# Another issue order for the attention stage, and six small instructions of the start on other engines

## The chip, the cores and the metric

The kernel runs on one core of one Trainium2 chip. The metric is the device time in microseconds (us) of one execution; the median of three runs is given for the kernel before. The core has five engines that run side by side, each with a queue that it works off strictly in order: TensorE (PE, matrix products and transposes; PEld is its weight load), VectorE (DVE), ScalarE (ACT), GpSimd (POOL) and SyncE (SP, which here only issues DMA transfers).

## The reference

Two stages, cut to what matters (B = 8 batches, H = 8 heads, S = 576 positions, D = 64, factor = 4, so 144 pooled positions):

```python
q_d = q.reshape(B, H, Sd, factor, D).mean(axis=3)   # k_d, v_d alike
out_d = sm_attn(q_d, k_d, v_d)                       # dense attention over 144 pooled positions
out_up = np.repeat(out_d, factor, axis=2)
mask = np.abs(pos[:, None] - pos[None, :]) < factor  # a band of 7 positions
attn = softmax(where(mask, scale * q @ k.T, -1e9))
x = out_up + attn @ v                                # -> 4608 tokens of 512 numbers
# second stage: each token goes to the best of 8 experts, if its skip score is above 0
h = np.maximum(xc[mask] @ w1[e], 0.0)
y[mask] = gate_w[mask, None] * (h @ w2[e])
out[do_compute] = xc + y
```

## The kernel before

**Attention.** The 4608 tokens are worked off in 36 tiles of 128 rows; a tile holds four groups of 32 positions with all 8 heads, and 4.5 tiles make a batch. A tile passes these steps, each a small function: `scores` (PE: four matmuls lay the mask into a PSUM bank `S`, 16 add the products), `s_max`, `s_sub` (DVE, from PSUM into `Et`), `s_exp` (ACT), `s_sum`, `recip` (DVE), `norm` (POOL, into `Nt`), `p_transpose` (PE), `p_evac` (ACT), `up_mm` and `values` (PE, into a bank `O`), `x_out` (ACT), `store_x` (a DMA), `x_transpose` (PE), `x_evac` (ACT), and the router's `logits`. Each batch also has its pooled attention: `pool_q`, `pool_k`, `pool_v` and `pool_vr` add four neighbours each, `d_scores` (PE, five of them into a bank `Sd`; n = 0 to 3 is a pair of heads each) is followed by `d_max` (DVE), `d_neg` and `d_exp` (ACT), `d_transpose`, `d_values` and so on. Each of the PSUM banks `S`, `Sd`, `T` and `O` exists twice: the third `scores` in the order waits until `s_sub` of the first has read its bank.

**Routing.** Every 16 tiles (and for the last four) the steps `r_...` count which token goes to which expert. `r_row` (DVE, L671) writes a tile `Am` that exists once, and `r_lists` (PE, 4 matmuls) reads it. At the end `slots` (L690) writes the list `gix`, and GpSimd gathers the first expert's rows by it. **The second stage** then runs expert by expert, written out in code that the change leaves alone.

**What sets the order.** All calls of the first stage, loads among them, are collected in a list of 1235 nodes (`node(...)`), and the table `ORDER` says in which order they are called. A manual schedule keeps that order on every engine and on the DMA queue of SP, so the table alone decides what stands in front of what. Semaphores are put in where data or a buffer asks for them.

The places that the change and the steps below touch: `pool_v` (L242 to L247) adds the four value rows of a batch in three adds; `pool_q0` (L260 to L272) pools the queries of batch 0, pairs 0 and 2 by one reduction on DVE and pairs 1 and 3 by three adds on POOL, and copies the last 16 columns behind the others; L766 is the helper `copy`, which casts the identity to `idb` and the mask to `mk`, both of which every `scores` needs; `zero_k` (L228, by `fill`, L184) zeroes the parts of the key buffers that no load writes, halves `hh` = 0 on ACT or DVE, 1 on POOL; `load_k` (L221), `load_q` (L208) and `load_v4` (L236) issue the loads, the first batch's keys in four pieces of 288 KB, its queries in two of 576 KB, its values in one of 512 and one of 640 KB.

```python
    def copy(eng, t, src):
        (eng.copy if eng is nc.scalar else eng.tensor_copy)(out=t, in_=src)
...
    for k in ORDER:
        fn, args = nodes[k]
        fn(*args)
```

Of the kernel before, what the change touches and what calls it, by code (L numbers as in the profile page):

```python
# [52 lines left out]


ORDER = (
# [61 lines left out]
)  # L117

@with_exitstack
def tile_attention_moe(ctx, tc, qT, kT, vW, v4, mask, cst, ups, cid, w9, w1, w2, out):
    nc = tc.nc
    NB = qT.shape[0]
# [114 lines left out]


    def pool_v(b, k):  # L242
        eng = nc.gpsimd if b else nc.vector
        if k == 0:
            B[b]["vd"] = dp.tile([128, D], F32, name="vd")
        vd, V4 = B[b]["vd"], B[b]["V4"][:, :4 * D].rearrange("p (r d) -> p r d", r=4)
        eng.tensor_add(out=vd, in0=V4[:, 0] if k == 0 else vd, in1=V4[:, k + 1])  # L247
# [21 lines left out]
        else:  # L269
            nc.gpsimd.tensor_add(out=qd, in0=qv[:, :, 0] if k == 0 else qd, in1=qv[:, :, k + 1])  # L270
        if k in (None, 2):
            eng.tensor_copy(out=s["qd"][:, p, SD:], in_=qd[:, 128:])  # L272

    def pool_q(b, k):
        s = B[b]
# [506 lines left out]
        node(load_q, 0, slice(2 * c, 2 * c + 2))  # L782
        for hh in range(2):
            node(load_k, 0, hh, 2 * c, 2)
    node(copy, nc.vector, idb, ident)
    node(copy, nc.scalar, mk, mkf)
    for i in range(2):
        node(fill, nc.scalar, VBs[0][:, i])
# [443 lines left out]
```

## Time and profile before

| what | us |
|---|---|
| runs: median (lowest to highest) of 3 | 467.70 (466.41 to 469.99) |
| the profiled execution, by its own time | 462.81 |
| its span, from the first to the last instruction | 461.0 |
| first matmul of TensorE | 10.84 |
| first list of rows (`gix`) written | 206.12 to 206.30 |

The profile is that of one execution. Its busy times are what an engine spends inside instructions; "idle <- X" and the waits name the instruction that ended an idle time. The attention stage runs from the start to about 206 us; the rest is the second stage.

### The profile page before, as it was taken

To read this page: it belongs to the slowest core of one execution; us is meant where nothing else is said; L and a number is where in the kernel's file an instruction comes from. 1 tells how busy PE (TensorE), PEld (TensorE's weight loads), DVE (VectorE), ACT (ScalarE), POOL (GpSimd) and SP (SyncE) were. 2 spreads that over 40 slices of the span, in tenths; PEclk is the share of its full clock that TensorE was granted. 3 is DMA by queue.
4 is the path that set the end of the run, shared out by engine and by line. 5 is a ranking of instruction groups with operands and counts; after the bars stand their busy time and mean duration, and the time that the engine had idled before them with its cause. 6 is when DMAs were issued, how large, how long until landed. Compare 5 with 4: busy or idle time off the path is not lost.

```text
span 461.0 us, 13595 instructions
## 1 busy us (share of the span) xinstructions
PE 431.7 (94%) x5593; PEld 368.7 (80%) x5593; DVE 314.2 (68%) x572; ACT 252.9 (55%) x583; POOL 170.0 (37%) x200
## 2 busy tenths in 40 slices
PE   0879999999899999989999999999999999999994
PEld 0657787787788688866989899898989898998993
DVE  5989999786888868774656556456776655666422
ACT  6666787878687787624643443343646334454320
POOL 8747884656838542107002204105040220201002
PEclk9999999999999999989999999999999999999999
DMA  8988888988887778636754644635667564455201
GB/s 276 323 262 280 282 268 276 309 260 304 273 279 213 221 228 257 206 129 179 256 159 153 226 143 138 240 113 206 240 207 240 199 224 138 164 179 186 91 3 57
DMA packets 27110, 96.67 MB, mean 210 GB/s; under 512 B 4245, under 2 KB 4629, under 8 KB 24618
## 3 DMA queue, kind: packets, MB, share of 16 engines
q1 hardware_dynamic: 23186, 84.36, 56.6%
q0 software_dynamic: 3840, 11.09, 6.4%
q8 instruction: 64, 1.05, 0.9%
q14 instruction: 20, 0.16, 0.1%
HBM read 81.20 MB, written 15.73 MB: 210 GB/s over the span
## 4 chain that ended last, share of the span: by engine, by line
issue 46%; PE 28%; POOL 9%; DVE 8%; DMA 4%; ACT 3%; POOLq 1%; SPq 0%; DVEq 0%
PE O L195 12%; PE T L198 7%; POOL xr L959 4%; PE Sd L195 4%; PE S L195 4%; POOL out L959 4%; DVE KD L288 2%; DMA cs<-cst 2%; DMA out<-Y,six 1%; DMA mkf<-mask 1%; ACT KB L186 1%; DVE nm L423 1%; ACT Ed L322 1%; POOL Nt L446 1%; DVE r L439 1%
## 5 line engine op out<-in xcount | busy, mean ns | idle before, releaser
L959 POOL DMA_INDIRECT out<-Y,six x24 | 24.3, 1011 | 190.8 <-DVE Y L1030 187.6
L993 PE MATMUL ph<-xth,w1h 128*128 128x384 f32 (+2 forms) x256 | 80.8, 316 | 0.7 <-PEq L1058 0.4
L993 PE MATMUL ph<-xth,w1l 128*128 128x384 f32 (+2 forms) x256 | 78.9, 308 | 0.0
L993 PE MATMUL ph<-xtl,w1h 128*128 128x384 f32 (+2 forms) x256 | 78.4, 308 | 0.0
L1022 PE MATMUL py<-w2h,hh 128*128 128x512 f32 (+1 forms) x168 | 64.9, 387 | 0.4
L1022 PE MATMUL py<-w2h,hl 128*128 128x512 f32 (+1 forms) x168 | 64.9, 386 | 0.0
L1022 PE MATMUL py<-w2l,hh 128*128 128x512 f32 (+1 forms) x168 | 64.9, 386 | 0.0
L1001 ACT ACTIVATE hh<-ph 128x384 fp32r<-128x384 f32 x64 | 30.9, 492 | 57.6 <-PE py L1022 26.5
L1002 DVE SCALAR_TENSOR_TENSOR hl<-ph,hh 128x384 fp32r<-128x384 f32 x64 | 34.6, 553 | 37.0 <-ACT hh L1001 35.3
L993 PEld LDWEIGHTS ph<-xth,w1h 128*128 128x128 f32 x256 | 48.1, 188 | 1.9 <-issue 1.6
L993 PEld LDWEIGHTS ph<-xtl,w1h 128*128 128x128 f32 x256 | 48.0, 188 | 0.4
L993 PEld LDWEIGHTS ph<-xth,w1l 128*128 128x128 f32 x256 | 48.1, 188 | 0.0
L710 DVE TENSOR_TENSOR w2l<-raw,w2h 128x1024 fp32r<-128x1024 f32 x32 | 39.1, 1221 | 10.5 <-ACT w2h L709 10.5
L288 DVE TENSOR_REDUCE KD<-KB 128x288 f32<-128x1152 f32 (+1 forms) x36 | 42.9, 1207 | 4.6 <-DMA KB<-kT 4.5
L983 ACT CAST xth<-Tx 128x512 fp32r<-128x512 f32 x22 | 12.9, 587 | 58.4 <-PE Tx L978 58.3
L748 DVE TENSOR_TENSOR w1l<-raw,w1h 128x1024 fp32r<-128x1024 f32 x30 | 36.7, 1224 | 7.9 <-ACT w1h L743 7.7
L709 ACT CAST w2h<-raw 128x1024 fp32r<-128x1024 f32 x32 | 33.6, 1051 | 14.4 <-PE py L1022 12.6
L446 POOL TENSOR_TENSOR Nt<-Et,r 128x304 f32<-128x304 f32 x36 | 26.1, 731 | 37.6 <-PE T L198 9.5
L984 DVE TENSOR_TENSOR xtl<-Tx,xth 128x512 fp32r<-128x512 f32 x22 | 15.2, 691 | 34.2 <-ACT xth L983 31.5
L195 PE MATMUL O<-VB,PT 126*32 126x128 f32 x1152 | 37.8, 275 | 0.3 <-issue 0.3
L1022 PEld LDWEIGHTS py<-w2h,hh 128*128 128x128 f32 x168 | 31.5, 188 | 6.7 <-issue 1.2
L1022 PEld LDWEIGHTS py<-w2h,hl 128*128 128x128 f32 x168 | 31.5, 188 | 6.5
(160 smaller groups left out, 937.3 us busy)
## 6 DMA issues: line engine op xcount, KB each, us to landing
raw<-w SPq DMA_DIRECT2D x62, 512.0 KB
VB<-vW SPq DMA_DIRECT2D x36, 336.0 KB
Q<-qT SPq DMA_DIRECT2D x16, 576.0 KB
out<-X SPq DMA_DIRECT2D x36, 256.0 KB
KB<-kT SPq DMA_DIRECT2D x14, 576.0 KB
V<-v SPq DMA_DIRECT2D x8, 640.0 KB
V<-v SPq DMA_DIRECT2D x8, 512.0 KB
KB<-kT SPq DMA_DIRECT2D x4, 288.0 KB
```

Source lines behind the costliest of these rows:

```text
L195: last[:] = [nc.tensor.matmul(*args, **kw)]
L198: last[:] = [nc.tensor.transpose(*args)]
L288: i = nc.vector.tensor_reduce(out=kd, in_=kv, axis=AX.X, op=ALU.add)
L446: nc.gpsimd.tensor_tensor(out=Ns[i % NNS][:, :, :KW, :2], in0=TT[i]["E"], in1=heads(TT[i]["r"])[:, :, None, :].to_broadcast([128, 4, KW, 2 ...
L709: nc.scalar.copy(out=hf, in_=raw)
L710: nc.vector.tensor_tensor(out=flat(lo), in0=raw, in1=hf.bitcast(F32), op=ALU.subtract)
L748: nc.vector.tensor_tensor(out=flat(lo), in0=raws[e, j], in1=flat(hi).bitcast(F32), op=ALU.subtract)
L959: ins = nc.gpsimd.indirect_dma_start(bounds_check=NOUT - 1, oob_is_err=False, **kw).ins
L993: nc.tensor.matmul(P[i][:, :n], lhsT=a[:, c, 128 * i:128 * i + 128], rhs=bb[:, c, :n], start=m == 0, stop=m == 11)
L1001: nc.scalar.activation(out=hh[:, i], in_=p, func=AF.Relu)
L1002: nc.vector.scalar_tensor_tensor(out=hl[:, i], in0=p, scalar=0.0, in1=hh[:, i].bitcast(F32), op0=ALU.max, op1=ALU.subtract)
L1022: nc.tensor.matmul(P, lhsT=a[:, i, ks], rhs=bb[:, i, cols], start=(j == 0 and i == 0 and m == 0), stop=(j == 3 and i == 1 and m == 2))
```

## The change

`ORDER` is another permutation of the same 1235 nodes, and three calls change their engine: `pool_v` of batch 0 from DVE to GpSimd (three adds), the two small copies of `pool_q0` that stood on DVE to ACT, and the cast of the identity from DVE to ACT.

```diff
 ORDER = (
-    5, 9, 0, 39, 37, 3, 4, 8, 12, 59, 61, 23, 21, 11, 2, 13, 38, 40, 58, 7, 57, 35, 55, 10, 46, 51, 60, 6, 1,
+    0, 8, 5, 3, 37, 4, 7, 11, 27, 60, 34, 10, 58, 16, 40, 9, 12, 57, 23, 61, 55, 6, 56, 1, 172, 28, 59, 18,
...
     def pool_v(b, k):
-        eng = nc.gpsimd if b else nc.vector
+        eng = nc.gpsimd
...
         if k in (None, 2):
-            eng.tensor_copy(out=s["qd"][:, p, SD:], in_=qd[:, 128:])
+            copy(nc.scalar if k is None else eng, s["qd"][:, p, SD:], qd[:, 128:])
...
-    node(copy, nc.vector, idb, ident)
+    node(copy, nc.scalar, idb, ident)
```

SP's queue at the start of the program, before (`Q`, `KB0`: queries and keys of batch 0; `mkf`: the mask; `V4`: values; `KB1` and the second `Q`: batch 1):

```order
L208 DMA Q_137<-qT 128x1152
L221 DMA KB0_116<-kT 64x1152 x3
L208 DMA Q_137<-qT 128x1152
L221 DMA KB0_116<-kT 64x1152
L763 DMA mkf_106<-mask 128x152
L208 DMA Q_174<-qT 128x1152
```

and after:

```order
L208 DMA Q_139<-qT 128x1152
L221 DMA KB0_116<-kT 64x1152 x2
L236 DMA V4_146<-v4 128x1024
L208 DMA Q_139<-qT 128x1152
L221 DMA KB0_116<-kT 64x1152 x2
L763 DMA mkf_106<-mask 128x152
```

The first half of the values now goes ahead of the second piece of queries and of the last two pieces of keys. The pieces of keys come in another order too: before (half, pairs) 1 of 0-1, 0 of 0-1, 1 of 2-3, then 0 of 2-3; after 1 of 2-3, 0 of 0-1, then 1 of 0-1, 0 of 2-3.

ScalarE's queue at the start, before (`mk`: the mask; `nmd`, `Ed`: `d_neg` and `d_exp`):

```order
L186 COPY KB_117<-zero 128x1216 x2
L186 COPY KB_116<-zero 128x1216
...
L766 CAST mk<-mkf 128x152
L186 COPY VB_118<-zero 126x2048
L311 ACTIVATE nmd<-nmd 128x2
```

and after:

```order
L186 COPY VB_118<-zero 126x2048
L766 COPY qd<-qd 128x16
L186 COPY KB_117<-zero 128x1216
L766 CAST mk<-mkf 128x152
L766 CAST idb<-ident 128x128
L311 ACTIVATE nmd<-nmd 128x2
```

The copy of pooled queries stands ahead of a zeroing and of the casts of the mask and the identity.

VectorE's queue at the start, before (`KD`: `pool_k`; `qd`: `pool_q0`; `nm`, `Et`: `s_max` and `s_sub`; `nmd`: `d_max`):

```order
L288 TENSOR_REDUCE KD_128<-KB_116 128x144 x2
L766 CAST idb<-ident 128x128
L288 TENSOR_REDUCE KD_128<-KB_116 128x144 x3
L268 TENSOR_REDUCE qd<-Q 128x144
L272 COPY qd<-qd 128x16
L288 TENSOR_REDUCE KD_128<-KB_116 128x144
L268 TENSOR_REDUCE qd<-Q 128x144
L272 COPY qd<-qd 128x16
L423 TENSOR_REDUCE nm<-S 128x8
L429 TENSOR_TENSOR Et_122<-S,nm 128x4x2x38
```

and after:

```order
L288 TENSOR_REDUCE KD_128<-KB_116 128x144 x7
L268 TENSOR_REDUCE qd<-Q 128x144
L288 TENSOR_REDUCE KD_128<-KB_116 128x144
L306 TENSOR_REDUCE nmd<-Sd 128x2
L423 TENSOR_REDUCE nm<-S 128x8
L429 TENSOR_TENSOR Et_120<-S,nm 128x4x2x38
```

Seven of the eight sums of keys stand ahead of the first sum of queries, and TensorE's first instruction is now the first `d_scores`, where it was the mask's matmul of the first `scores`. The `scores` of the first tiles come in the order 2, 0, 1, 3, 4, 5 before and 0, 2, 1, 3, 4, 6, 5 after.

VectorE's queue in the last routing, before (`Am`: `r_row`; `oh`: `r_hot`; `sl`: `r_slot`, `r_own`; `s_all`: `r_place`):

```order
L592 TENSOR_TENSOR oh<-eq,pm 128x36
L671 TENSOR_TENSOR Am<-cs,smod 128x512
L629 TENSOR_TENSOR sl<-Sd,BT 128x36
L638 TENSOR_TENSOR sl<-sl,oh 128x36
L643 TENSOR_REDUCE s_all<-sl 128x4
```

and after:

```order
L592 TENSOR_TENSOR oh<-eq,pm 128x36
L671 TENSOR_TENSOR Am<-cs,smod 128x512
L629 TENSOR_TENSOR sl<-Sd,BT 128x36
L638 TENSOR_TENSOR sl<-sl,oh 128x36
L671 TENSOR_TENSOR Am<-cs,smod 128x512
L643 TENSOR_REDUCE s_all<-sl 128x4
```

A second `Am` of the routing of tiles 16 to 31 now stands between the steps of the last one; on TensorE its four matmuls stand behind the last `logits1` where they stood ahead of it.

## Rows read from the trace of the kernel before

**Rows 1.** The page, part 1: busy us (share of span) xinstructions

```profile
PE 431.7 (94%) x5593; PEld 368.7 (80%) x5593; DVE 314.2 (68%) x572; ACT 252.9 (55%) x583; POOL 170.0 (37%) x200
```

**Rows 2.** Stretches of the span: busy time of each engine, clock, DMA share, GB/s

```profile
core 0: us, PE busy (x) PEld busy (x) DVE busy (x) ACT busy (x) POOL busy (x), PEclk, DMA share, GB/s
0.00:30.00 30.00, 16.54 (x334) 11.36 (x338) 24.15 (x51) 19.99 (x51) 24.07 (x39) 1.00 0.89 298
30.00:70.00 40.00, 37.60 (x904) 29.65 (x894) 36.81 (x76) 29.17 (x97) 28.45 (x30) 1.00 0.82 268
70.00:200.00 130.00, 126.74 (x2919) 104.67 (x2917) 104.73 (x234) 97.20 (x280) 65.60 (x82) 1.00 0.81 259
200.00:210.00 10.00, 8.09 (x52) 4.37 (x52) 6.93 (x32) 1.35 (x6) 2.89 (x4) 0.66 0.16 52
```

**Rows 3.** TensorE's waits, 30 to 210 us, then 0 to 30: total, times, longest

```profile
PE Sd L195 <- DVE KD L288: 1.7, 2, 1.1
PE S L195 <- issue: 1.6, 1, 1.6
...
PE S L195 <- ACT mk L766: 10.8, 1, 10.8
...
PE T L198 <- POOL Nt L446: 0.2, 1, 0.2
```

**Rows 4.** Timeline of the start: start us, us, engine, line, operation

```profile
2.04 3.41 ACT L186 COPY KB<-zero 128x1216 f32<-128x1216 f32 x3
...
5.99 0.59 SPq L763 DMA_DIRECT2D mkf<-mask  x1
...
6.71 1.41 DVE L288 TENSOR_REDUCE KD<-KB 128x144 f32<-128x576 f32 x2 [4.53 <-DMA KB<-kT]
...
8.17 2.06 DVE L288 TENSOR_REDUCE KD<-KB 128x144 f32<-128x576 f32 x3
...
10.47 0.32 ACT L766 CAST mk<-mkf 128x152 bf16<-128x152 f32 x1 [3.21 <-DMA mkf<-mask]
...
15.86 0.70 PE L195 MATMUL S<-KB,Q 128*32 128x76 f32 x32
...
16.52 0.72 PE L195 MATMUL Sd<-KD,qd 128*128 128x288 f32 x2
...
18.32 0.46 DVE L429 TENSOR_TENSOR Et<-S,nm 128x304 f32<-128x304 f32 x1
...
18.70 0.46 DVE L423 TENSOR_REDUCE nm<-S 128x8 f32<-128x304 f32 x1
```

**Rows 5.** DMA from 0 to 60 us in 40 slices of 1.5 us

```profile
GB/s 0 151 304 258 372 401 358 410 453 384 237 312 394 259 245 252 287 351 275 259 374 197 44 276 380 335 171 180 347 375 168 378 403 292 281 305 193 169 190 342
```

**Rows 6.** Groups of 0 to 206 us: DVE, then ACT, then POOL

```profile
L247 DVE TENSOR_TENSOR vd<-vd,V 128x512 f32<-128x512 f32 x2 | 1.9, 930 | 0.0
...
L247 DVE TENSOR_TENSOR vd<-V 128x512 f32<-128x512 f32 x1 | 1.0, 1004 | 0.0
...
L272 DVE COPY qd<-qd 128x16 f32<-128x16 f32 x2 | 0.7, 332 | 0.1
...
L766 DVE CAST idb<-ident 128x128 bf16<-128x128 f32 x1 | 0.2, 216 | 0.0
...
L610 ACT CAST pcs<-gf 128x16 bf16<-128x16 f32 x4 | 0.9, 235 | 0.6 <-DVE gf L616 0.6
...
L247 POOL TENSOR_TENSOR vd<-vd,V 128x512 f32<-128x512 f32 x14 | 18.4, 1313 | 9.4 <-DMA V<-v 6.7 <-DVE rd L373 2.1
```

**Rows 7.** Timeline of the last routing

```profile
202.62 0.68 DVE L671 TENSOR_TENSOR Am<-cs,smod 128x512 bf16<-128x512 f32 x1
...
203.78 0.61 PE L195 MATMUL Sd<-Bm,Am 128*128 128x120 bf16 x4
...
204.43 0.69 DVE L671 TENSOR_TENSOR Am<-cs,smod 128x512 bf16<-128x512 f32 x1
...
206.12 0.18 DVE L690 TENSOR_TENSOR gix<-Sd,ids 128x24 int32<-128x24 f32 x1
```

118 rows, old and new, of the table ORDER are left out of this document.

## Prediction

> **What bounds the kernel now.** The page's first part comes first: TensorE is busy for 94% of the span, VectorE for 68%, ScalarE for 55% [rows 1]. The mean hides two regimes, so the second view is the stretches [rows 2]. From 70 to 200 us TensorE is busy for 126.74 of 130 us and no other engine comes near. In the first 30 us it has 16.54, while VectorE has 24.15, ScalarE 19.99 and GpSimd 24.07. TensorE's idle time in the attention stage is thus 13.46 us to 30, 2.40 us from 30 to 70, 3.26 us from 70 to 200 and 1.91 us from 200 to 210. The change issues the same matmuls and transposes, so nearly all that it can move is these 21 us. The third view is TensorE's waits [rows 3]: 10.8 us is the first wait, for the mask's cast on ScalarE; later single waits are 1.7 us for sums of keys and 1.6 us that no engine ends. The timeline of the start [rows 4] shows that the mask was cast the moment its load landed (the cast starts at 10.47 after 3.21 us of waiting), and that VectorE worked from 6.71 on, when the first keys had come.
>
> **Step 1: the first matmul, now behind keys and queries.** TensorE's first row needs the key sums of pair 0 (both halves) and the query sum of pair 0. The last load among these is the sixth: 576 + 288 + 288 + 512 + 576 + 288 = 2528 KB must have landed. Before, the mask was the last of 2 x 576 + 4 x 288 + 76 = 2380 KB and was there at 10.44, just ahead of its cast [rows 4]. The slices around 10 us move 358 and 410 GB/s [rows 5], so 148 KB more is 0.4 us: 10.9. VectorE has done three sums by then, and five of its instructions stand from there to the query sum; three sums took 2.06, so 5 x 0.69 = 3.4, and the first matmul starts at 14.4. Bounds: were all loads early, eight sums from about 7.5 would end at 13.0; were the piece as late after its issue as the mask was (5.99 to 10.44, and GpSimd's zeroings let it be issued at about 5.8, an estimate), nothing changes; I keep 13.0 to 15.5.
>
> **Step 2: ScalarE's queue stops behind the copy.** The copy of the pooled queries that moves to ScalarE waits for the sum that ends at 14.4. Behind it in order stand a zeroing of keys (3.41 for three, so 1.14 [rows 4]), the mask's cast (0.32) and the identity's. The identity's cast is not in the trace of ScalarE: its nearest rows are the mask's cast at 0.32 and a 16-column cast at 0.235 [rows 6]; I take 0.3, and 0.24 for each copy. The mask and the identity, that every score row needs, are so ready at 14.4 + 0.24 + 1.14 + 0.32 + 0.3 = 16.4, though the mask lands at about 12. TensorE has only its first pooled score to do, 0.7 [rows 4], up to 15.1, and waits 1.3.
>
> **Step 3: two stops at the score banks.** The fourth score row (tile 3) needs the bank that VectorE's `s_sub` of tile 2 frees. VectorE gets the first bank at 17.6 (a first score row takes about 1.2) and has up to that `s_sub` ten small steps of 0.38 (two starts in a row: 18.32 and 18.70 [rows 4]), a query sum of 0.69, a sum of values of about 0.5 and a reciprocal of about 0.1: 22.8. TensorE has three more pooled rows and two score rows to do (3 x 0.55 + 2 x 0.85) and is through at about 20.9, so it waits 2.0. The seventh score row (tile 5) needs the `s_sub` of tile 4, behind six small steps and a key sum of twice the size (1.4) that start when tile 3's scores are there at 23.8: 27.5. TensorE does four items, 2.7 us, and waits 1.1. Its idle time is then 14.4 + 1.3 + 2.0 + 1.1 = 18.8 us at 28 us, where before it had 13.46 up to 30: +5.3. With the bounds of step 1, +3.9 to +6.4.
>
> **Step 4: VectorE's relief.** VectorE loses three adds (1.9 + 1.0), two copies (0.7) and a cast (0.2): 3.8 us [rows 6], against 60.96 us that it works in the first 70 [rows 2]. GpSimd gets three adds of 1.3 (the same operation in the other batches [rows 6]): 3.9 us; ScalarE 0.8 us, counted above. Since TensorE comes 5 us late to the stretch from 30 to 70 us and VectorE only some 2, most of the 2.40 us that TensorE idled there has no cause left. I take 1.9 back; all of it is the best case, and 3 us more of waiting the worst, since VectorE has waited for ScalarE in step 2 too.
>
> **Step 5: the rest of attention.** Of the 3.26 us from 70 to 200 the longest wait for a key sum is 1.1 [rows 3], which the new order has no reason to repeat: -1.1. The 1.6 that no engine ended I leave as it is. Bounds: 0 and -3.3.
>
> **Step 6: the last routing.** Four `r_lists` matmuls (0.37) move behind the last `logits1`: -0.4. In return a second `r_row` stands between the steps of the last routing, and since `Am` exists once it waits for the matmuls that before end at 203.78 + 0.61 = 204.39 [rows 7]. It would end at 205.1, where before the next `r_row`, the one that the list needs, started at 204.43. What stands between the two in the new order (five small steps of about 0.15 and the wait for the second set of matmuls, 0.5 from 205.1) puts that one at 205.9, so the list comes 1.5 us later: +1.1 in sum. Bounds: 0 and +1.5.
>
> **The sum.** 5.3 - 1.9 - 1.1 + 1.1 = +3.4 us. The profiled execution, 462.81, would become 466.2. Its span is 461.0, 1.8 us less than its time, and it lies 4.9 below the median of the runs, 467.7, to which I add the difference: 471.1. The ends of the steps add up to -1.8 and +10.9, so 465.9 to 478.6.
>
> **Rivals.**
> First, TensorE's rows of 126.74 in 130 us hide slack. Its weight loads are busy for 104.67 of the same 130 us [rows 2], so 25.3 us lie between them. If short waits sit inside the matmuls' recorded time and a VectorE that is less pressed gives back a third, 8.4 us, the time is 471.1 - 8.4 = 462.7. For it speaks that loads and matmuls differ by 22 us there; against it that matmuls with many columns take longer than their loads in any order, and that VectorE has 25 us free in that stretch already. The Trainium skill, "Perfetto Trace Analysis", section "Identifying the Most-Contended Engine", says the same of the two rows: matmul busy time is no good measure of what is left, the share of the weight loads is. By that rule the headroom is 19.5% of the stretch, where by the matmul row it is 2.5%. The trace can't tell which of it an order can win.
>
> Second, GpSimd becomes the early bound, the case on the other side. It has 24.07 us of work in the first 30 [rows 2] and gets 3.9 us more, ahead of the first `norm`. The `norm` of a tile stands before its transpose on TensorE, and before the change that wait cost 0.2 us in all of the start [rows 3]. If GpSimd is through with the adds so late that TensorE's first transposes wait the 3.9 us in full, the time is 471.1 + 3.9 = 475.0. It decides when GpSimd idles for less than 2 us of its first 30. Against it: the adds need values that land by about 15 us, when GpSimd would otherwise wait for data.
>
> Third, the start is not later than its loads: pieces land sooner, the waits in step 3 overlap with work that I counted one after the other, and the first 30 us cost 1.5 in place of 5.3: 467.3, no change.
>
> **How the numbers follow.** A measurement of this kernel tells about 1%, 4.7 us, from no change. The forecast has 0.48; its own range is 467.5 to 474.5, of which I put 0.30 within 1% and 0.18 above. The first rival has 0.13 (0.11 below by over 1%, 0.02 within), the second 0.22 (0.19 above, 0.03 within), the third 0.17 (0.03 below, 0.13 within, 0.01 above). That makes 0.14 faster, 0.48 the same, 0.38 slower. The range reaches from 463.5, just above the first rival's time, to 478.0, past the second's and near the upper end of the sum.
>
> **What would show it.** Right: TensorE's first matmul is a pooled score at about 14.4 and its first score row comes at about 16.4, behind an ScalarE that waited for VectorE's `qd`; TensorE's idle time is about 19 us in the first 30 and under 1 us from 30 to 70; a second `Am` stands in the last routing and waits for TensorE. Wrong: a first matmul before 12 or a mask's cast before 13 takes steps 1 and 2 away; waits for `Nt` of several us mean the second rival; a busy time of TensorE from 70 on that shrinks with its matmuls unchanged means the first.

## The result, and the profile after

| | before | after |
|---|---|---|
| runs: median (lowest to highest) of 15 | 466.65 (463.12 to 470.29) | 473.98 (467.95 to 478.91) |
| ratio of after to before, 95% interval | | 1.0144 (1.0109 to 1.0178) |
| the profiled execution, own time | 462.81 | 473.98 |
| its span | 461.0 | 472.2 |
| list of rows `gix` begins to be written | 206.12 | 217.17 |

The change costs 1.4%, 6.7 us by the ratio. The ratios, here and below, leave out executions that took over 1.5% longer than the fastest of their kernel, so they need not match the medians. From the list on both profiles are alike: the span less the time of `gix` is 472.2 - 217.17 = 255.0 and 461.0 - 206.12 = 254.9. So all of the loss lies in the attention stage. The two profiled executions differ by 11.2 us, more than the medians, since that of before is one of its faster ones; a part of what follows is therefore larger between these two profiles than between typical runs.

The page of after, part 1, beside [rows 1]:

```profile
PE 435.7 (92%) x5593; PEld 371.9 (79%) x5593; DVE 307.2 (65%) x566; ACT 252.8 (54%) x586; POOL 173.4 (37%) x203
```

The instructions went where the change sent them, VectorE is busy 7 us less, and TensorE 4 us more with as many matmuls. The stretches of the kernel after, beside [rows 2]; the columns are the same:

```profile
core 0: us, PE busy (x) PEld busy (x) DVE busy (x) ACT busy (x) POOL busy (x), PEclk, DMA share, GB/s
0.00:30.00 30.00, 12.68 (x275) 8.33 (x276) 17.93 (x34) 15.51 (x38) 20.24 (x32) 1.00 0.74 249
30.00:70.00 40.00, 38.23 (x873) 29.83 (x874) 37.13 (x81) 32.20 (x105) 31.07 (x36) 1.00 0.86 287
70.00:200.00 130.00, 123.36 (x2850) 101.31 (x2846) 97.03 (x223) 93.51 (x276) 69.06 (x77) 0.99 0.80 248
...
86.80:90.20 3.40, 3.40 (x29) 2.31 (x31) 1.21 (x4) 2.56 (x9) 0.25 (x1) 0.50 0.35 143
```

Subtract the busy time from the length and compare. TensorE idles 17.3 us in the first 30 (before 13.5), 1.8 from 30 to 70 (2.4), and 6.6 from 70 to 200 (3.3). The last row is one short stretch in which TensorE's granted clock was 0.50, the lower of its two levels (1.2 GHz); from 30 to 200 us before had none.

The start of the kernel after, beside [rows 4]:

```profile
6.79 2.07 DVE L288 TENSOR_REDUCE KD<-KB 128x144 f32<-128x576 f32 x3 [4.61 <-DMA KB<-kT]
12.22 2.73 DVE L288 TENSOR_REDUCE KD<-KB 128x144 f32<-128x576 f32 x4 [3.36 <-POOL qd L270]
...
15.64 0.20 ACT L766 COPY qd<-qd 128x16 f32<-128x16 f32 x1 [9.49 <-DVE qd L268]
15.66 1.33 PE L195 MATMUL Sd<-KD,qd 128*128 128x288 f32 x2 [15.66 <-DVE qd L268]
15.76 1.20 ACT L186 COPY KB<-zero 128x1216 f32<-128x1216 f32 x1
16.86 0.31 ACT L766 CAST mk<-mkf 128x152 bf16<-128x152 f32 x1
17.08 0.29 ACT L766 CAST idb<-ident 128x128 bf16<-128x128 f32 x1
17.42 0.45 PE L195 MATMUL S<-mk,idb 128*32 128x304 bf16 x4 [0.43 <-ACT idb L766]
17.65 1.24 PE L195 MATMUL S<-KB,Q 128*32 128x76 f32 x32
18.82 1.33 PE L195 MATMUL Sd<-KD,qd 128*128 128x288 f32 x2
...
20.30 1.23 PE L195 MATMUL S<-KB,Q 128*32 128x76 f32 x32
...
23.59 0.31 PE L195 MATMUL S<-mk,idb 128*32 128x304 bf16 x4
...
28.90 0.31 PE L195 MATMUL S<-mk,idb 128*32 128x304 bf16 x4 [0.91 <-DVE Et L429]
```

Read it downwards as a queue. VectorE's fourth sum of keys is ready to go only at 12.22; the name behind the arrow is misleading there, since that sum needs a load and a zeroing of GpSimd that was over long before, and the transfer's last part landed at 12.13. The query sum ends at 15.6, ScalarE's copy waits 9.49 us for it, and behind the copy stand the zeroing, the mask's cast and the identity's. The first score row starts at 17.42, 1.76 us behind the first matmul. The products of that row take 1.24 us. Those of the first row of before, at 11.06, took as long, and later ones 0.70, at 15.86 [rows 4]; the clock column shows 1.00 for the first 30 us of both, so why TensorE's first rows are slow isn't shown. The fourth score row, at 23.59, starts without a wait.

TensorE's waits from 30 to 220 us, beside [rows 3]:

```profile
PE T L198 <- issue: 3.7, 2, 2.2
PE O L195 <- issue: 2.3, 4, 0.9
PE S L195 <- issue: 1.1, 3, 0.7
...
PE Sd L195 <- DVE Am L671: 0.8, 1, 0.8
```

"issue" is a wait that no engine and no transfer of data ends. These are 7.1 us; before there were 3.0, of which [rows 3] shows 1.6. The waits for sums of keys that led the list before are gone. The last routing, beside [rows 7]:

```profile
211.26 0.19 DVE L562 TENSOR_REDUCE mx<-Sd 128x4 f32<-128x32 f32 x1 [0.82 <-PE Sd L195]
...
212.28 0.69 DVE L671 TENSOR_TENSOR Am<-cs,smod 128x512 bf16<-128x512 f32 x1
214.11 0.69 DVE L671 TENSOR_TENSOR Am<-cs,smod 128x512 bf16<-128x512 f32 x1 [0.81 <-PE Sd L195]
...
215.47 0.69 DVE L671 TENSOR_TENSOR Am<-cs,smod 128x512 bf16<-128x512 f32 x1
217.17 0.18 DVE L690 TENSOR_TENSOR gix<-Sd,ids 128x24 int32<-128x24 f32 x1
```

The second `Am` stands there and waits for TensorE. From the first step of the last routing (`mx`) to `gix` it takes 5.9 us, before 4.5.

**Where 11 us went.** To 30 us TensorE idles 3.9 us more; from 30 to 70 it idles 0.6 less; from 70 to 200 it idles 3.4 more; the last routing takes 1.4 more; and TensorE is busy 3.0 us longer for the same matmuls (up to the last routing 185.5 us, before 182.5). The stretch at half clock explains up to 1.7 of that, and a second one, from 209.7 on, up to 0.8 ahead of the last routing, both estimates from the lengths of the stretches. The sum is 11.1, `gix` comes 11.05 later.

### The profile page after: what moved, and what is told of

It reads as the page before. It is cut to its first block, busy times and chain, and to the rows that moved or that the text cites. A ratio compares the mean times of both kernels' runs of the same rounds, so it can differ in the third digit from the quotient of the medians.

```text
span 472.2 us, 13582 instructions
## 1 busy us (share of the span) xinstructions
PE 435.7 (92%) x5593; PEld 371.9 (79%) x5593; DVE 307.2 (65%) x566; ACT 252.8 (54%) x586; POOL 173.4 (37%) x203
## 3 DMA queue, kind: packets, MB, share of 16 engines
q8 instruction: 64, 1.05, 0.9%
## 4 chain that ended last, share of the span: by engine, by line
issue 46%; PE 33%; POOL 9%; DVE 5%; DMA 4%; ACT 1%; POOLq 1%; SPq 0%; DVEq 0%
PE O L195 14%; PE T L198 9%; PE Sd L195 5%; PE S L195 5%; POOL xr L959 4%; POOL out L959 3%; DMA V<-v 3%; DVE KD L288 1%; DMA out<-Y,six 1%; DVE nm L423 1%; DVE Et L429 1%; DVE rd L373 0%; DVE nmd L306 0%; PE S L910 0%; DVE r L439 0%
## 5 line engine op out<-in xcount | busy, mean ns | idle before, releaser
L195 PE MATMUL Sd<-KD,qd 128*128 128x288 f32 (+1 forms) x128 | 28.6, 433 | 16.0 <-DVE qd L268 15.7
L709 ACT CAST w2h<-raw 128x1024 fp32r<-128x1024 f32 x32 | 33.6, 1051 | 14.4 <-PE py L1022 12.6
L195 PE MATMUL O<-VB,PT 126*32 126x128 f32 x1152 | 38.9, 275 | 2.3 <-issue 2.3
```

The lines of the kernel that those rows point to most:

```text
L195: last[:] = [nc.tensor.matmul(*args, **kw)]
L709: nc.scalar.copy(out=hf, in_=raw)
```

## The experiments

**The parts: order alone, engines alone.** One kernel has the new table with the old engines, one the old table with the new engines. (In some of the kernels below a line's number is 1 to 3 lower than in after, and L763 is the helper that is L766 there.) Order alone is the kernel before with

```diff
 ORDER = (
-    5, 9, 0, 39, 37, 3, 4, 8, 12,
+    0, 8, 5, 3, 37, 4, 7, 11, 27,
...
```

> The new order with the six instructions on their old engines (the identity's cast, the two copies and the three sums of values on VectorE). First theory (the start: ScalarE's queue stops behind the copy): the mask's cast no longer waits for the query sum and starts when its load lands, about 12 to 13 us; VectorE carries 3.8 us more in the first 70, so the first score row comes at about 16.5 and tile 3's at 24 or later; total about 470 to 474, 3 to 7 above before. Second theory (the middle: TensorE waits for blocks of its own program, the waits that no engine ends): the engines of six instructions change nothing there, such waits are again 4 to 8 us between 30 and 210, and the total is 472 to 476. Rival (it is the engines, not the order): within 2 us of before.

Measured: 475.26 (470.07 to 476.05), ratio to before 1.0185 (1.0125 to 1.0246). The order alone makes the whole loss. The mask's cast started at 11.91, the first matmul at 14.38 and the first score row at 16.39, as the first theory wanted, though the time, 474.3 by the ratio, lies just above its 470 to 474; the waits that no engine ends were 7.8 us from 30 to 200, as the second wanted.

```profile
10.93 2.73 DVE L285 TENSOR_REDUCE KD<-KB 128x144 f32<-128x576 f32 x4 [1.90 <-DMA KB<-kT]
...
11.91 0.32 ACT L763 CAST mk<-mkf 128x152 bf16<-128x152 f32 x1 [4.65 <-DMA mkf<-mask]
```

In these rows of the timeline of order alone, the same sums of keys start at 10.93 on the same loads in the same order. The parts of that transfer landed between 9.56 and 10.84 here and between 10.2 and 12.13 in the profile of after: its last part came 1.3 or 1.9 us behind its first. Five other runs with the same first loads had the last part at 10.9, 11.3, 11.4, 12.0 and 12.4, so this differs from one execution to the next, with the sums of values on GpSimd in each of the five.

Engines alone is the kernel before with

```diff
-        eng = nc.gpsimd if b else nc.vector
+        eng = nc.gpsimd
...
-            eng.tensor_copy(out=s["qd"][:, p, SD:], in_=qd[:, 128:])
+            copy(nc.scalar if k is None else eng, s["qd"][:, p, SD:], qd[:, 128:])
...
-    node(copy, nc.vector, idb, ident)
+    node(copy, nc.scalar, idb, ident)
```

> The old order with the six instructions on their new engines. First theory: here too ScalarE's copies wait for VectorE's query sums, but in the old order they stand elsewhere in ScalarE's queue; the loss is 0 to 2 us, total 465 to 469. Second theory: no loss from the engines, 466 to 468, with waits that no engine ends of about 3 us as before. Rival (the engines): 470 to 474, with the whole loss here.

Measured: 469.52 (465.5 to 474.98), ratio 1.0077 (1.0035 to 1.0118): the engines alone cost 3.6 us in the old order, which no theory gave. ScalarE's timeline in engines alone, of an execution of 474.37, says where:

```profile
10.49 0.20 ACT L763 COPY qd<-qd 128x16 f32<-128x16 f32 x1 [4.83 <-DVE qd L265]
11.81 0.20 ACT L763 COPY qd<-qd 128x16 f32<-128x16 f32 x1 [1.12 <-DVE qd L265]
11.92 1.89 ACT L183 COPY VB<-zero 126x2048 f32<-126x2048 f32 x1
13.72 0.31 ACT L763 CAST mk<-mkf 128x152 bf16<-128x152 f32 x1
```

The two copies wait for VectorE; a zeroing of 1.89 us that before ran at 5.36, while the mask was still on its way, now runs behind them, and the mask's cast behind that. A copy of 0.2 us has cost the first score row 2 to 3 us (before: cast at 10.47 [rows 4], in the second profile below at 11.84). To see that it is the copies, the next kernel leaves these two on VectorE:

```diff
-            copy(nc.scalar if k is None else eng, s["qd"][:, p, SD:], qd[:, 128:])
+            eng.tensor_copy(out=s["qd"][:, p, SD:], in_=qd[:, 128:])
```

> The old order with two of the three engine changes: the sums of the first batch's values on GpSimd and the identity's cast on ScalarE; the copies of pooled queries stay on VectorE. With the copies too (measured: 1.0077 of before) the mask's cast came at 13.7 instead of 10.5. First theory: the copies alone made that loss; here the cast is at 10.5 again and the time within 1 us of before, 465 to 467. Rival: the sums on GpSimd delay the first norms or the loads, and the loss stays: 469 to 470.

Measured: 466.6 (462.41 to 472.61), ratio 1.0020 (0.9977 to 1.0063), no change. The mask's cast starts the moment its load lands:

```profile
11.60 0.32 ACT L763 CAST mk<-mkf 128x152 bf16<-128x152 f32 x1 [4.15 <-DMA mkf<-mask]
```

So of the engine changes, the copies cost (1.0077 - 1.0020, some 2.7 us, the intervals overlapping a little), and the sums on GpSimd neither cost nor gain what can be measured.

**Start against middle.** Two kernels splice the tables: the first 200 steps of one, then what is left in the order of the other.

```diff
+ORDER = before[:200] + [k for k in after if k not in before[:200]]     # old start
+ORDER = after[:200] + [k for k in before if k not in after[:200]]      # new start
```

> The first 200 of the 1235 steps in the old order, the rest in the new one, the new engines. It takes the new start away and leaves the new middle and the new last routing. First theory (start +5.3, last routing +1.1): about 1.4 above before, 468; TensorE idles 13 to 14 us in the first 30. Second theory (start +3.3 in the profile, last routing +1.4, the rest in the middle by waits for program): 3 to 7 above before, 470 to 474, and between 70 and 200 us TensorE idles about 6 us, of which 4 or more end by no engine.

> The first 200 steps in the new order, the rest in the old one, the new engines. It has the new start and the old middle and last routing. First theory: about 4 to 5 above before, 471; TensorE idles 17 us in the first 30 and the first matmul comes at 15 to 16. Second theory: +3 from the start alone, about 469.5, and between 70 and 200 us TensorE idles 3 to 4 us as before.

Measured: old start 478.5 (474.75 to 482.93), ratio 1.0266 (1.0201 to 1.0331), more than either theory gave; new start 475.25 (469.05 to 478.53), ratio 1.0130 (1.0056 to 1.0203), 471.7 by the ratio, which fits the first and, by its interval, the second. TensorE of old start idled 16.8 us in its first 30, where the first theory had 13 to 14, and 7.3 from 70 to 200, where the second had about 6; TensorE of new start idled 17.4 in its first 30 with its first matmul at 15.91, as the first theory had it, and 7.4 from 70 to 200, where the second had 3 to 4. The waits of old start from 30 to 200 us show why it tells little:

```profile
PE O L192 <- issue: 3.4, 4, 1.3
PE O L192 <- DVE rd L370: 3.4, 1, 3.4
...
PE T L195 <- POOL vd L244: 2.1, 1, 2.1
```

The seam makes waits of its own (5.5 us for `rd` and `vd`, which neither parent has), and so does that of the other splice (1.6 us for values that are still on their way). These two runs don't separate the parts.

**Undoing one step in the new order.** First the last routing, with `r_row` and `r_lists` of three groups back where they stood:

```diff
-r_row(4) ... r_max, r_skip ... r_lists(4) ... r_row(8), r_slot, r_lists(8), r_own, r_row(12), r_place ... r_lists(12)
+r_row(4), r_lists(4), r_row(8), r_max, r_skip, r_lists(8) ... r_row(12), r_lists(12), r_slot, r_own, r_place
```

> The changed kernel with the steps r_row and r_lists of tiles 20, 24 and 28 put back to their old places about the last routing; nothing else differs. By step 6 of the prediction the stretch from r_max to gix shrinks by 1.4 us, from 5.9 in the changed kernel to about 4.5, no second Am stands between r_slot and r_block, and the time falls by 1.1 to 1.4 us, to about 472.5. If the sets of matmuls that come ahead of the last logits push these back by as much, the stretch shrinks and r_max comes later, and the time stays at 474. Rival (the last routing waits for something else): gix still 5.9 us behind r_max.

Measured: 472.4 (469.1 to 474.89), ratio 1.0192 (1.0144 to 1.0239). In the timeline the stretch shrinks from 5.9 to 4.7, where about 4.5 was expected:

```profile
207.71 0.18 DVE L559 TENSOR_REDUCE mx<-Sd 128x4 f32<-128x32 f32 x1
...
212.42 0.18 DVE L687 TENSOR_TENSOR gix<-Sd,ids 128x24 int32<-128x24 f32 x1
```

The time does not show it: a gain of 1.2 us is a quarter of a per cent, and the intervals of the two kernels (1.0109 to 1.0178 and 1.0144 to 1.0239) are wider than that. The mechanism is shown, its price in the time is not.

Then the copies, back on VectorE in the new order:

```diff
-copy(nc.scalar if k is None else eng, s["qd"][:, p, SD:], qd[:, 128:])
+eng.tensor_copy(out=s["qd"][:, p, SD:], in_=qd[:, 128:])
```

> The changed kernel with the two copies of pooled queries back on VectorE; the sums of values stay on GpSimd and the identity's cast on ScalarE. By step 2 ScalarE no longer stops: mask's cast when its load has landed, at about 12 to 13 us, identity right behind it, and the first score row 0.7 us behind the first matmul (1.8 in the changed kernel). The first matmul stays at 14.4 to 15.7, since it hangs on the sixth load and VectorE's sums. Gain about 1 us, less 0.35 that VectorE gets back before the scores: total 473. Rival (the queue behind the copy was the main loss of the start): gain of 3 us or more, 471 or less. Of the sixth load: at 12.2 us in the changed kernel and at 10.9 with the sums of values on VectorE; if the sums on GpSimd make it late, it is late here too; if it was that execution, 10.9.

Measured: 471.95 (470.08 to 479.48), ratio 1.0175 (1.0126 to 1.0224): no gain that can be measured. The mask's cast came at 11.87, and still the first score row stood 1.25 us behind the first matmul (14.45 and 15.70, 1.76 in after), for the pooled score is itself 1.33 long there, where 0.7 had been taken [rows 4]. In the new order ScalarE's stop costs 0.5, since the query sum, which is late by itself, holds TensorE anyway; in the old order it costs 2 to 3.

**A second profile of before.**

> The kernel before once more, unchanged, for a second profile of it. The first one's execution, 462.8, lies 3.9 us under the median of the runs. If TensorE's waits that no engine ends belong to an order, they are again about 3 us between 30 and 210 us, and this profile differs elsewhere. If they differ from one execution to the next, an execution of 466 to 468 has 6 to 8 us of them, as the changed kernel (7.1) and the four kernels measured so far (6.6 to 8.3) had.

Measured: 463.65. The waits that no engine ends were 2.3 us from 30 to 200, as few as in the first profile. The mask's cast came at 11.84, 1.4 us later than in [rows 4], so that TensorE idled 14.7 us in its first 30 and not 13.5; the span is 461.9 against 461.0. Here are those waits, of before again and of the run with the old last routing, which is the kernel after up to about 200 us:

```profile
PE S L195 <- issue: 1.8, 1, 1.8
PE T L198 <- issue: 0.5, 1, 0.5
```

```profile
PE O L192 <- issue: 2.7, 5, 1.1
PE T L195 <- issue: 1.9, 1, 1.9
```

This execution of before is again faster than the median, and one of 466 to 468, which was to decide, did not come. The other profiles tell more. In the old order the kernel without the copies had 3.4 us of such waits at 467.43, and engines alone 8.3 at 474.37. In the new order the run with the old last routing had 4.6 at 469.1, after 7.1 at 473.98, order alone 7.8 at 476.05, and the run with the copies back on VectorE 12.4 at 479.48. So the waits differ from one execution to the next within an order, and the slower executions mostly have more of them. The new order has more in executions near the median (7.1 against 3.4) and in the fastest (4.6 against 2.3 and 3.0), but with one or two profiles of each kernel it is not shown how much of that belongs to the order.

**What ends these waits.** The trace counts matmuls, and these waits stand at a certain spacing. Here are the stretches from 0 to just ahead of a wait, of after (three), before, before again and the kernel without the copies (one each); the first number in brackets counts the matmuls:

```profile
0.00:62.30 62.30, 43.23 (x980) 31.64 (x981) 48.62 (x102) 42.34 (x128) 46.98 (x62) 1.00 0.81 273
0.00:86.11 86.11, 64.82 (x1488) 49.55 (x1488) 68.39 (x140) 58.77 (x178) 61.90 (x79) 1.00 0.83 273
0.00:111.12 111.12, 88.42 (x1995) 68.39 (x1995) 84.50 (x177) 74.82 (x224) 75.06 (x93) 0.98 0.81 263
```

```profile
0.00:124.16 124.16, 106.54 (x2502) 83.25 (x2502) 105.19 (x220) 91.06 (x277) 86.66 (x107) 1.00 0.86 284
```

```profile
0.00:124.76 124.76, 106.12 (x2502) 83.14 (x2502) 105.82 (x220) 91.21 (x277) 86.89 (x107) 1.00 0.86 283
```

```profile
0.00:126.69 126.69, 107.29 (x2502) 83.36 (x2502) 104.03 (x216) 91.20 (x278) 89.44 (x110) 1.00 0.85 280
```

1488 - 980 = 508 = 4 x 127; 1995 - 1488 = 507 and 2502 - 1995 = 507, each 4 x 127 but for one. Each of these numbers leaves 89 to 91 when divided by 127. A matmul of these rows is two instructions, its weight load and itself, so 127 of them are 254 instructions, and the third part of the profile's page has a queue "q8 instruction" with 64 packets and 1.05 MB, 16.4 KB each. The longest wait of after, in the timeline of weight loads:

```profile
86.12 0.31 PEld L198 LDWEIGHTS T<-ident,Nt 128*126 128x126 f32 x3 [2.44 <-issue]
```

And the DMA queues of after in the half microsecond, 83.5 to 84, in which that wait began (packets, MB, share of the 16 engines):

```profile
q1 hardware_dynamic: 63, 0.12, 63.8%
q8 instruction: 1, 0.02, 13.4%
```

One packet of q8 starts at 83.7, and TensorE goes on 2.4 us behind its start, in the middle of four transposes of one tile. In the 15 waits of its weight loads of 0.7 us or more from 30 to 200 us of after, before, before again, the kernel without the copies and before with the shift below, it goes on 2.3 to 2.9 us behind the start of such a packet. The reading: TensorE's own program comes in packets, one for each 127 matmuls or so, which the profile counts on the same 16 DMA engines as the data, and when a packet starts later than 2.4 us ahead of the end of the block before it, TensorE runs dry. From 30 to 200 us a packet starts 1.9 us (before) and 2.5 us (after) behind the first matmul of the block that runs, as means over 30 packets each; it is 2.1 in before again and 2.3 in the run with the old last routing, so the two orders lie close.

To test this, 63 matmuls of one element were put ahead of TensorE's first, in time in which it waits for the first loads; they shift the program by half a block and leave the order of the work as it is.

```diff
         fn(*args)
+        if k == 0:
+            t = psS.tile([128, 512], F32, name="S")
+            for _ in range(63):
+                nc.tensor.matmul(t[:1, :1], lhsT=zero, rhs=zero, start=True, stop=True)
```

> The kernel before with 63 matmuls of one element ahead of its first, in time in which TensorE has nothing to do (they end by about 8 us; its first own one came at 10.8 to 12.2). They shift the program against its blocks of 127 matmuls by half a block. Theory: the waits that no engine ends stand again at counts that leave 90 when divided by 127, the 63 counted, so at other places of the work than before; no wait of over 1 us at the old place (matmul 2565 with the 63 counted). Where they fall is not foreseen: the time is between 466 and 472. Rival (the place in the work makes the wait, not the block): it is at matmul 2565, and the time is 466.

Measured for before with the shift: 468.92 (465.83 to 476.46), ratio 1.0036 (0.9994 to 1.0078). Nothing waits at 2565 any more. Two of its five waits, first in the timeline of weight loads, then as the stretches up to them:

```profile
77.37 0.57 PEld L192 LDWEIGHTS S<-KB,Q 128*32 128x32 f32 x18 [2.81 <-issue]
...
128.18 0.16 PEld L192 LDWEIGHTS S<-KB,Q 128*32 128x32 f32 x8 [1.62 <-issue]
```

```profile
0.00:77.36 77.36, 62.62 (x1488) 48.08 (x1488) 67.63 (x142) 54.64 (x162) 55.29 (x72) 1.00 0.87 282
0.00:128.17 128.17, 111.29 (x2630) 87.69 (x2630) 104.78 (x220) 91.45 (x277) 86.35 (x107) 0.99 0.85 275
```

1488 and 2630 leave 91 and 90 again, with the 63 counted, so in the work they stand half a block from where they stood. The wait follows the block, not the work.

> The changed kernel with the same 63 matmuls ahead of its first (its first own one came at 14.4 to 15.7). Theory: the six waits leave their places; with other places the middle has 2 to 13 us of them, and the time is between 467 and 477; if the order was bad only by its alignment with the blocks, 468. Rival: the six waits stay with the work, at counts 63 higher, and the time stays at 473.

Measured for after with the shift: 474.0 (472.37 to 477.49), ratio 1.0182 (1.0121 to 1.0242). Its six waits stand at other places too (the first three at matmuls 1108, 1616 and 1996, leaving 91 or 92), and 7.9 us of such waits are left. So the alignment alone doesn't make the new order bad: with another one it waits as long.

Last, 32 of the 36 loads of windowed values were left out of both kernels, to see whether the packets are late because of the loads. The tiles from the fifth on then use the values of the first ones again, so the tokens go to other experts and the second stage takes another time (916.64 and 909.39 in all); only the attention stage can be compared.

```diff
     def load_v(n, r):
+        if n > 1:
+            return
```

> The changed kernel without the loads of the windowed values of tiles 4 to 35 (32 of 36 transfers of 336 KB; the values of the first four tiles are used again, so the output is another). Theory (TensorE waits for the next 16 KB of its program, whose packet stands behind the loads): the waits at matmuls 981, 1488, 1868, 1995, 2504 and 3390 shrink to under 1 us in sum where they are 5 to 13 in the changed kernel and its near relatives, no stretch at half clock between 30 and 200, and the time falls by 4 to 7 us, to 466 to 469. Rival (the waits don't come from the loads, or the middle is slow for another reason): within 2 us of 473.

> The kernel before without the same 32 loads. Theory: it has only one such wait, at matmul 2502, of 1.8 to 2.0 us, to lose, so it gains 2 to 3 us: 462 to 464; and the difference between the two kernels without these loads is what the start and the last routing cost, 3 to 5 us. Rival: the difference between the two stays at 7 us.

Measured, up to `gix`: after without these loads 215.16 (with them 217.17), before without them 203.25 (206.12 and 207.30 with them). The waits that no engine ends from 30 to 200 us, of after without the loads; of before without them there is no such row:

```profile
PE T L195 <- issue: 2.8, 2, 2.0
PE O L192 <- issue: 2.8, 3, 2.3
...
PE S L192 <- issue: 0.4, 2, 0.2
```

The wait at 2502 of before is gone, as the theory had it. Of after 6.0 us of 7.1 are left, the three longest at two of the old places and a new one, where the theory had wanted less than 1. The difference between the orders, 11.9 us here, has not shrunk to 3 to 5. By these two executions the loads make some of the packets late and are not what makes the new order worse; which transfers are was not tried any further.

## Why the prediction was right, and where not

The time lies inside the range and on the side of the forecast; the single figure, +3.4 us, is half of what was measured, +6.7, and this makes the kernel slower by over 1%, which had 0.38, where within 1% had 0.48. By its steps:

- **Step 1** (first matmul at 14.4 behind the sixth load at 10.9): the sum was right, with 14.38 and 10.93 in the run of the order alone, 15.66 and 12.2 in the profile of after. The term that was mis-sized is the landing: the parts of this transfer land 1.3 to 2.1 us apart, and how far differs from one execution to the next.
- **Step 2** (ScalarE's queue stops behind the copy, TensorE waits 1.3): seen as described, 1.76 from first matmul to first score row. But the pooled score, put at 0.7 from a later row [rows 4], takes 1.33 at this place, so that the wait for the identity is 0.43 and not 1.3, and putting the copies back showed 0.5 for the whole stop in this order. In the old order, where nothing else holds TensorE, it is worth 2 to 3 us and shows in the time (1.0077 against 1.0020).
- **Step 3** (two stops at the score banks, 18.8 us idle at 28): idle time 17.3 in the first 30; the stop ahead of tile 5 is there, 0.91, but the one ahead of tile 3, put at 2.0, is not. TensorE comes to that row at 23.59 and not at 20.9, because the pooled row at 18.82 and the score row at 20.30 take 1.33 and 1.23, where 0.55 and 0.85 were taken. The first matmul, in return, was 1.3 later than forecast. That the two errors left +3.9 of +5.3, the lower bound, is in part luck; against the second profile of before it is +2.6, below the bound.
- **Step 4** (1.9 given back from 30 to 70): 0.6 was. What still idles there is mostly waits for program (1.0 of 1.8).
- **Step 5** (-1.1 in the rest, "the 1.6 that no engine ended I leave as it is") is the step that failed. The waits for key sums went, as it said. But those that no engine ends were left out of the sum as a thing that an order does not touch, and between the two profiles it is just these that went from 3.0 to 7.1, with a stretch at half clock behind the longest. (How much of that is the order and how much the execution stays open, as said above.) The row was in [rows 3] and its cause could have been looked for in the trace: the count of matmuls ahead of it and the queue q8. From 70 to 200 us TensorE idles 3.4 more and not 1.1 less. TensorE's busy time, which the sum took as unchanged, grew by 3.0.
- **Step 6** (+1.1 in the last routing): +1.4 by the profile, and the undone kernel takes 1.2 of it away in the trace; the time does not show it.

How the 6.7 us of typical executions divide is not measured. As an estimate, the start costs 2.6 (17.3 - 14.7, against the second profile of before) and the last routing 1.4, so 2.7 is left for the middle, in waits for program and in longer busy time. Between the first two profiles the start has 3.9 and the middle 5.8, since that execution of before is one of its faster ones.

**The rivals.** Slack in TensorE's rows: nothing of it: its busy time grew with the matmuls unchanged. By the Trainium skill, "Perfetto Trace Analysis", section "Identifying the Most-Contended Engine", TensorE's headroom is judged by the busy share of the weight loads and by the operations done, not by the matmuls' row. No run here shows an order that wins any of it: from 70 to 200 us the weight loads' row fell from 104.67 to 101.31 us of 130, with fewer loads done in it (2846 for 2917), and the kernel became slower. GpSimd as the early bound: it idled 9.8 of the first 30 us, far from the 2 at which that was to decide, and TensorE waited 0.4 for `Nt`. A start of +1.5: no, +3.9 against the first profile of before and +2.6 against the second.

What stays open: what makes packets of program late, since the loads of windowed values are only a part of it, and whether the new order makes them later in every execution (2.3 and 2.5 us behind their block against 1.9 and 2.1). No version beat the kernel before; the nearest is the one that leaves out the copies and the order, 1.0020.

## What to carry to other kernels

Before an instruction moves to an idle engine, read what is queued behind it there: a copy of 0.2 us that waits for another engine holds up all that follows, and the price is the wait, not the copy. A wait that no engine ends can be explained: count the instructions up to it, and where the counts have a common spacing, suspect that the engine waits for its own program. Such waits change their places when the program is shifted, and their lengths from one execution to the next, so take more than one profile of each kernel before they are put down to an order. The same holds for the base of a forecast: the profile of before that this one started from had loads that landed over 1 us earlier than those of the next one. A stage that idles for 3 us in 130 has little to win and much to lose, so for a new order of such a stage the forecast should lean to slower.

## What the runs showed of the hardware that had not been expected

- In the attention stage TensorE's program comes in packets of 16.4 KB on the queue "q8 instruction", one for about 127 matmuls with their weight loads; TensorE goes on about 2.4 us behind the start of a packet it waits for, and single waits were up to 3.4 us (new start, at 136.8 us).
- After TensorE's wait of 2.20 us in after, its granted clock was 0.50, the lower level, from 86.8 to 90.2, which can cost up to 1.7 us on top of the wait (half of the stretch, an estimate). Of the twelve waits for program of 2.0 us or more in all profiles nine came with a stretch at 0.50, and three did not (2.49 and 2.50 us with the copies back on VectorE, 2.27 in after without the loads).
- The first and the last part of the same load of 288 KB landed 1.3 to 2.1 us apart in different executions, and its last part at 10.8 to 12.4 us, which moved the first matmul by over 1 us (14.38 to 15.66).
